# A list scheduler's task priorities: a table of ranks in place of positions from formulas, in an attention and softplus MLP kernel

## The chip, the cores and the metric

The kernel runs on one core of a Trainium2 chip, as one program. The metric is the device time of one execution in microseconds (us), the median of a few runs. The profile is one execution taken by the hardware profiler; it lists every instruction of the engines PE (TensorE matmuls), PEld (its weight loads), DVE (VectorE), ACT (ScalarE), POOL (GpSimd) and SP (the queue that issues nearly all DMAs).

## The reference

Two blocks follow each other. The first is a linear attention with an RMS norm for 8 batches, 8 heads, 576 positions and head size 64; the second is an MLP with softplus over the 4608 tokens that come out.

```python
kv  = einsum('bhsd,bhse->bhde', k, v)
o   = einsum('bhsd,bhde->bhse', q, kv)
a   = o / sqrt(mean(o*o, axis=-1) + 1e-6) * g_norm
x   = a.transpose(0, 2, 1, 3).reshape(4608, 512)
h   = x @ w_in                       # w_in  512 x 2048
g   = max(h, 0) + log1p(exp(-abs(h)))
out = g @ w_out                      # w_out 2048 x 512
```

## The kernel before, in words

**Numbers in three parts.** The MLP's matmuls take operands that are split into three parts (`high`, `low`, `less`), so that three matmuls stand for one. Every operand is split once, by one ACT and two DVE instructions. The weights come in as 64-bit words and are turned into floats first, by six DVE and two ACT instructions for each of 32 pieces (`weight`, lines 409 to 477: `square`, `high1`, `high2`, `mask`, `beyond`, `power`, `rest`, `total`), and are then split (`split_weight`, lines 486 to 538). For the first four of the 16 chunks of the hidden dimension, PE does one step of that split (`less_by_pe`, lines 518 to 521).

**The attention.** `kv_of` (lines 662 to 700) loads k and v of a batch in five pairs and multiplies them on PE (line 691); ACT copies the result (line 699). `rows` (lines 702 to 826) does a tile of 128 tokens: q turned round (on PE at line 771 for batches 0 and 1, on DVE at line 746 for the others), q times kv on PE (`out_rows`, line 715), squares on ACT (line 788), a sum on DVE (`reduce`, line 719), the root on POOL (`root`, lines 722 and 723), and the product on DVE (`norm`, line 727). The first 12 tiles are turned round on PE (`turn_x`, line 733). The first six tiles of x are split at once from PSUM; the others go to DRAM and come back (`x_again`, line 833) before `split` (lines 623 to 649, DVE lines 638 and 641) cuts them.

**The MLP, phase 0.** Tokens go in 12 blocks of 384 (three tiles). A `step` (lines 844 to 892) does one block and one chunk of 128 hidden units: `mm1` (12 matmuls of 384 columns, line 858), softplus and `high` on ACT (lines 880 and 882), `low` and `less` on DVE (lines 869 and 873), and three `mm2` tasks of three matmuls of 512 columns (line 865). Blocks 0 to 3 do chunks 0 to 3, blocks 4 to 11 do chunks 0 to 5: 64 steps.

**The MLP, phases 1 and 2.** The other chunks are done for blocks of 512 tokens in 48 `wide_step`s (lines 1038 to 1161): seven products of six matmuls (line 1060), with copies, additions and softplus on ACT and DVE between them, then eight `mm2` tasks of three matmuls (line 1130). Sums of a phase leave PSUM through ACT (line 925), go to DRAM (`leave`) and come back (`enter`). `leave` of the very last tile of tokens is cut in two halves that ACT (line 915) and DVE (line 918) bring out, with two stores, one issued by SP (line 922) and one by ACT (line 923).

**What sets the order.** Nothing is issued where it stands in the source. Each piece of work is handed to a `Plan` as one of 3795 tasks (`add`, line 79), with its engine, a cost in ns, the tasks that it comes after, the buffers that it takes and gives back, and a position `pos`. `order` (lines 90 to 198) then plays the whole program through: at each turn it takes, for every engine, the tasks that are free to start, keeps those that could start within 0.15 us (`SOON`) of the earliest, and of these chooses the one with the smallest `pos`. The engine whose choice can start first gets it. The list of tasks in order of planned start is the program; each engine works through its part in that order. `pos` is a number from formulas with fitted constants: the step, plus offsets for each kind of task (the lists P0 to P7, lines 250 to 258, `x_pos` at line 657, and the offsets in each helper). Three more rules stand beside `pos`: 64-wide matmuls of one kind (`kv` or `rows`) are kept together and a change of kind is charged on PE; a DMA's `behind` names the `mm1` or first product after which it may be issued; and where PE would stand idle before the seventh `mm1`, the plan puts in a filler matmul of the identity (`warm`, line 1224).

Of the kernel before, what the change touches and what calls it, by code (L numbers as in the profile page):

```python
# [21 lines left out]
DOWN = 1.0 - 2.0 ** -13  # L22
DOWN_G = 1.0 - 0.99 * 2.0 ** -13
E = 1.0 / RADIX


def shaped(x, shape, dtype):
# [28 lines left out]
class Plan:  # L56
# [22 lines left out]
    def add(self, engine, ns, run, after=(), pos=0.0, take=(), give=(), size=0, behind=None, follows=None, kind="all"):  # L79
        pos, behind = round(pos, 4), None if behind is None else round(behind, 4)  # L80
        t = Task(engine, ns, run, [a for a in after if a is not None], pos, list(take), list(give), size)
        for s in t.give:
            s.readers += 1
        self.tasks.append(t)
        t.follows = follows
        t.behind = behind
        t.kind = kind
        return t
# [113 lines left out]
def kernel(  # L202
# [120 lines left out]
    plan = Plan(rings, heirs)  # L323
# [162 lines left out]
    def split_weight(w, part_of, n, dst, ready, pos, of_in, by_pe=False):  # L486
# [28 lines left out]
        def third():  # L515
            nc.scalar.activation(dst.tile[:, 2], d.tile, func=AF.Copy, scale=-E / (1.0 + E))

# [5 lines left out]
        def third_of_bank():  # L523
            nc.scalar.activation(dst.tile[:, 2], bank.tile, func=AF.Copy, scale=-E / (1.0 + E))

# [318 lines left out]
    def step(s):  # L844
# [26 lines left out]
        def less():  # L871
# [7 lines left out]
        mm1s.append((s, a))  # L879
        a = add("ACT", 490, lambda: nc.scalar.activation(new(g, [P, NT]), h.tile, func=AF.Softplus, scale=1.0 + E),  # L880
                [a], s, [g], [h])
# [156 lines left out]
    def wide_step(k):  # L1038
# [47 lines left out]
        def softplus(dst, src):  # L1086
            nc.scalar.activation(dst, src, func=AF.Softplus, scale=1.0 + E)  # L1087

# [76 lines left out]
    def whole_scale(pos):  # L1165

        if not wide:
            scale_done.append(add("DVE", 60, lambda: nc.vector.memset(scale, 1.0 + E), (), pos))
            return
# [5 lines left out]
        scale_done.append(add("ACT", 200, lambda: nc.scalar.activation(  # L1175
            scale, total.tile[:, 0, :1], func=AF.Copy, scale=(1.0 + E) * 2.0 ** -30 / (P * 2 * KF * d_model)), [a], pos, [], [total]))

# [47 lines left out]
                         start=True, stop=True)  # L1225

    plan.spare = ("h", warm, 400, mm1s[6][1])
    for t in plan.order():
        t.run()

# [29 lines left out]
```

## Time and profile before, and how to read it

| | before |
|---|---|
| median of 3 runs | 869.63 us (868.54 to 869.97) |
| span of the profiled execution | 867.5 us |
| PE busy | 853.9 us, 98% |
| DVE busy | 704.4 us, 81% |
| ACT busy | 521.3 us, 60% |
| POOL busy | 76.6 us, 9% |
| HBM read and written | 112.98 and 52.95 MB |
| filler matmuls (line 1224) | 52 |

The span runs from the first to the last instruction of the profiled execution; the time of a run is measured from outside and is some 2 us more. A busy time is the union of an engine's instructions. A matmul's end is modelled, so a busy PE may still work below its pace; the distance between the starts of two matmuls tells more than their length. In a timeline, the bracket at the end of a line gives the engine's idle time before that instruction and what ended it.

### The profile page before, as it was taken

The page shows a single profiled execution, that of the slowest core. Times are in us where ns is not written, and L with a number is a line of the kernel's source. Part 1 is how long each engine was busy: PE and PEld are TensorE (multiplying, and loading weights), DVE is VectorE, ACT ScalarE, POOL GpSimd, SP SyncE. Part 2 cuts the span into 40 slices and gives each one's busy share as a digit, 9 for nine tenths or more (in the row PEclk, how much of TensorE's full clock was granted, in tenths as well). Part 3 has the DMA queues.
Part 4 walks back from the last instruction along what each step waited for, and adds up shares of the span by engine and source line. Part 5 has one row for each costly group of instructions (what it writes and reads, how often), then busy time and mean ns, then how long its engine had stood idle before and what let it go on. Part 6 is the DMA issues. An engine that isn't in the chain of part 4 may idle for free.

```text
span 867.5 us, 17041 instructions
## 1 busy us (share of the span) xinstructions
PE 853.9 (98%) x6464; PEld 760.3 (88%) x6464; DVE 704.4 (81%) x995; ACT 521.3 (60%) x980; POOL 76.6 (9%) x79
## 2 busy tenths in 40 slices
PE   7899999999999999999999999999999999999998
PEld 5678888898888999989999999998999899999996
DVE  7888898888788879798887798878788666788873
ACT  6866664445444467766667655654868555566654
POOL 0342223111113200000000000000000000000000
PEclk9999999999999999999999999999999999999999
DMA  9998998779773655436645546545364752777764
GB/s 278 285 242 230 244 262 255 172 224 234 211 188 114 180 175 166 145 108 209 210 156 164 168 151 205 188 144 170 122 201 140 230 165 91 241 236 241 242 190 126
DMA packets 239778, 167.07 MB, mean 193 GB/s; under 512 B 106320, under 2 KB 198736, under 8 KB 239696
## 3 DMA queue, kind: packets, MB, share of 16 engines
q1 hardware_dynamic: 239392, 165.86, 64.5%
q8 instruction: 50, 0.82, 0.4%
q14 instruction: 32, 0.26, 0.1%
q10 hardware_dynamic: 304, 0.13, 0.1%
HBM read 112.98 MB, written 52.95 MB: 191 GB/s over the span
## 4 chain that ended last, share of the span: by engine, by line
PE 94%; DVE 1%; ACT 1%; POOL 0%; issue 0%; ACTq 0%; DVEq 0%
PE banks L1130 31%; PE banks L1060 28%; PE banks L865 16%; PE banks L858 15%; PE banks L715 2%; PE banks L691 2%; PE banks L733 0%; DVE units L638 0%; DVE half L727 0%; PE banks L1224 0%; POOL roots L723 0%; DVE units L641 0%; DVE roots L719 0%; DVE m L459 0%; ACT units L635 0%
## 5 line engine op out<-in xcount | busy, mean ns | idle before, releaser
L1130 PE MATMUL banks<-pieces,gv 128*128 128x512 f32 x768 | 239.9, 394 | 0.0
L1130 PEld LDWEIGHTS banks<-pieces,gv 128*128 128x128 f32 x768 | 133.5, 189 | 18.4
L1130 PE MATMUL banks<-pieces,g_False 128*128 128x512 f32 x384 | 149.4, 389 | 0.0
L858 PE MATMUL banks<-units,pieces 128*128 128x384 f32 x768 | 145.4, 337 | 0.0
L865 PE MATMUL banks<-pieces,gv 128*128 128x512 f32 x576 | 144.9, 396 | 0.0
L858 PEld LDWEIGHTS banks<-units,pieces 128*128 128x128 f32 x768 | 135.5, 188 | 4.8
L865 PEld LDWEIGHTS banks<-pieces,gv 128*128 128x128 f32 x576 | 106.1, 188 | 20.3
L1060 PEld LDWEIGHTS banks<-units,pieces 128*128 128x128 f32 x840 | 112.8, 190 | 6.8 <-ACT banks L1105 0.4
L1060 PE MATMUL banks<-units,pieces 128*128 128x256 f32 x840 | 117.1, 282 | 0.0
L880 ACT ACTIVATE half<-banks 128x384 f32<-128x384 f32 x64 | 31.4, 491 | 98.2 <-PE banks L858 98.0
L1120 DVE TENSOR_TENSOR gv<-g_True,gv 128x1024 fp32r<-128x1024 f32 x47 | 57.5, 1223 | 37.8 <-ACT gv L1117 37.8
L1130 PEld LDWEIGHTS banks<-pieces,g_False 128*128 128x128 f32 x384 | 72.2, 188 | 15.9
L1060 PEld LDWEIGHTS banks<-units,w 128*128 128x128 f32 x504 | 67.8, 190 | 3.9 <-ACT banks L1105 0.2
L1060 PE MATMUL banks<-units,w 128*128 128x256 f32 x504 | 70.7, 282 | 0.0
L723 POOL TENSOR_TENSOR roots<-roots,half 128x8 f32<-128x8 f32 x36 | 62.3, 1731 | 3.0
L1123 DVE SCALAR_TENSOR_TENSOR g_False<-gv 128x1024 fp32r<-128x1024 f32 x47 | 57.6, 1225 | 1.5
L1109 DVE TENSOR_TENSOR g_True<-banks,g_True 128x512 f32<-128x512 f32 x48 | 33.1, 690 | 30.5 <-PE banks L1060 24.5
L1087 ACT ACTIVATE g_True<-banks 128x256 f32<-128x256 f32 x96 | 36.6, 382 | 32.8 <-PE banks L1060 32.2
L1023 DVE TENSOR_TENSOR units<-loads,units 128x1024 fp32r<-128x1024 f32 x42 | 51.2, 1219 | 6.3 <-ACT units L1020 6.3
L925 ACT ACTIVATE m<-banks 128x512 f32<-128x512 f32 x72 | 42.1, 595 | 19.8 <-PE banks L1130 13.8
L1026 DVE SCALAR_TENSOR_TENSOR units<-units 128x1024 fp32r<-128x1024 f32 x42 | 51.4, 1224 | 1.8
L869 DVE TENSOR_TENSOR gv<-half,gv 128x384 fp32r<-128x384 f32 x64 | 35.4, 553 | 20.6 <-ACT gv L882 19.9
(115 smaller groups left out, 1260.5 us busy)
## 6 DMA issues: line engine op xcount, KB each, us to landing
loads<-x SPq DMA_DIRECT2D x180, 128.0 KB, 2.6
part<-m SPq DMA_DIRECT2D x72, 256.0 KB, 2.9
m<-part SPq DMA_DIRECT2D x72, 256.0 KB, 3.2
loads<-form SPq DMA_DIRECT2D x45, 256.0 KB, 3.2
form<-loads SPq DMA_DIRECT2D x36, 256.0 KB, 3.0
raw<-in_moe_w_in_dram SPq DMA_DIRECT2D x16, 512.0 KB, 4.5
loads<-in_k_dram SPq DMA_DIRECT2D x32, 256.0 KB, 4.1
loads<-in_v_dram SPq DMA_DIRECT2D x32, 256.0 KB, 4.4
```

The source lines that it names most:

```text
L723: nc.gpsimd.tensor_tensor(out=r.tile, in0=r.tile, in1=half, op=ALU.pow)
L858: nc.tensor.matmul(hp, lhsT=w_in.tile[:, i, kd * P:(kd + 1) * P], rhs=xv.tile[:, i, kd], start=(m == 0), stop=(m == 3 * KD - 1))
L865: nc.tensor.matmul(mine[i].tile, lhsT=gv.tile[:, m, i * P:(i + 1) * P], rhs=w_out.tile[:, m], start=(c == cs[0] and m == 0), stop=(c == cs ...
L869: nc.vector.tensor_tensor(out=gv.tile[:, 1], in0=g.tile, in1=gv.tile.bitcast(F32)[:, 0], op=ALU.subtract)
L925: a = add("ACT", 690 if ph == LAST else 600, lambda: nc.scalar.activation(new(ot, [P, d_model]), bank.tile, func=AF.Copy, scale=scale if p ...
L1023: nc.vector.tensor_tensor(out=part_of(1, F32R), in0=xl.tile if m > 1 else xl.tile[:, 0], in1=part_of(0), op=ALU.subtract)
L1026: nc.vector.scalar_tensor_tensor(out=part_of(2, F32R), in0=part_of(1), scalar=-RADIX, in1=part_of(0), op0=ALU.mult, op1=ALU.add)
L1060: nc.tensor.matmul(place(q), lhsT=w[:, m, at:at + P], rhs=dst.tile[:, m, v, kd] if u < 6 else dst.tile[:, m, kd], start=(u == 0 and not m ...
L1087: nc.scalar.activation(dst, src, func=AF.Softplus, scale=1.0 + E)
L1120: nc.vector.tensor_tensor(out=gvt(1, F32R), in0=gt(), in1=gvt(0), op=ALU.subtract)
L1123: nc.vector.scalar_tensor_tensor(out=gt(F32R), in0=gvt(1), scalar=-RADIX, in1=gvt(0), op0=ALU.mult, op1=ALU.add)
L1130: nc.tensor.matmul(mine[i].tile, lhsT=(gvt(m, F32R) if m < 2 else gt(F32R))[:, c, i * P:(i + 1) * P], rhs=outs[c].tile[:, m], start=fresh ...
```

## The change

Before the plan is ordered, each task's `pos` is replaced by a number from a table `RANK` of 3795 integers, one for each task in the order in which the source adds them. The integers are the numbers 0 to 3794, each once. Everything else of the plan stays: costs, dependencies, buffers, the rule of `SOON`, `behind`, `follows`, the rule for 64-wide matmuls and the filler's. The same 3795 tasks come out in another order; only the number of fillers, which the ordering itself puts in, can differ.

```diff
+RANK = [
+    0, 7, 6, 8, 10, 16, 13, 15, 18, 22, 26, 31, 38, 42, 1, 19, 20, 23, 29, 34, 32, 37, 40, 44, 48, 53, 58, 60, 17, 47, 43, 45, 50, 56, 54, 57, 63, 65, 78,
...
+    3774, 3704, 3707, 3718, 3751, 3738, 3752, 3746, 3758, 3747, 3750, 3756, 3760, 3759, 3764, 3762, 3766, 3767, 3769, 3773, 3771, 3776, 3783, 3777, 3781,
+    3779, 3782, 3784, 3787, 3792, 3794, 3780, 3786, 3791, 3785, 3788, 3789, 3793, 3790,
+]
...
     plan.spare = ("h", warm, 400, mm1s[6][1])
+    assert len(RANK) == len(plan.tasks)
+    for t, at in zip(plan.tasks, RANK):
+        t.pos = at
     for t in plan.order():
         t.run()
```

## The prediction

> **What bounds the kernel now.** I read the stages first, to see where any engine has time to lose. The columns are PE, PEld, DVE, ACT and POOL busy (instructions), the granted clock, the DMA share and GB/s.
>
> ```profile
> 0.00:44.00 44.00, 35.66 (x463) 25.53 (x464) 36.70 (x66) 31.27 (x60) 10.10 (x17) 1.00 1.00 281
> 44.00:84.00 40.00, 38.52 (x465) 32.26 (x464) 35.05 (x61) 27.25 (x55) 14.05 (x13) 1.00 0.92 225
> 84.00:137.00 53.00, 53.00 (x545) 46.90 (x544) 47.32 (x82) 31.86 (x63) 13.88 (x14) 1.00 0.87 240
> 137.00:357.00 220.00, 220.00 (x1830) 198.00 (x1829) 185.05 (x319) 116.38 (x230) 38.59 (x37) 1.00 0.68 188
> 357.00:863.70 506.70, 506.70 (x3169) 457.59 (x3167) 399.78 (x470) 314.11 (x573) 0.00 (x0) 1.00 0.57 179
> ```
>
> From 84 to 863.7 us PE has no gap. That this is its pace and not only modelled ends, the starts show: from one wide step to the next it is 10.53 us throughout, 42 matmuls of 256 columns at 0.12 us and 24 of 512 at 0.23. No order makes these shorter. So time can be won or lost in three places: before about 84 us, where PE stands still for 9.8 us and spends about 12 us on fillers (52 at the 0.23 us of a filler among others); in PE's detours to 64-wide matmuls; and after the last matmul.
>
> Next, what feeds PE in the early part. A block of phase 0 can start its first `mm1` when DVE has split its last tile. At blocks 2, 3 and 4 that is just in time (line 641 is the end of the split):
>
> ```profile
> 93.29 0.69 DVE L641 SCALAR_TENSOR_TENSOR units<-units 128x512 fp32r<-128x512 f32 x1
> ...
> 94.17 2.27 PE L858 MATMUL banks<-units,pieces 128*128 128x384 f32 x12
> ...
> 115.55 0.69 DVE L641 SCALAR_TENSOR_TENSOR units<-units 128x512 fp32r<-128x512 f32 x1
> ...
> 115.93 1.40 PE L858 MATMUL banks<-units,pieces 128*128 128x384 f32 x7
> ...
> 136.05 0.68 DVE L641 SCALAR_TENSOR_TENSOR units<-units 128x512 fp32r<-128x512 f32 x1
> ...
> 136.87 0.87 PE L858 MATMUL banks<-units,pieces 128*128 128x384 f32 x4
> ```
>
> So the bound up to 137 us is DVE's queue as much as PE: a PE that came earlier would wait there. At the later blocks the split is done 0.9 to 5.5 us ahead. DVE itself loses time by waiting in its order. Its waits from 35 to 137 us, by what ended them (total, times, longest):
>
> ```profile
> DVE roots L719 <- ACT half L788: 3.9, 4, 1.2
> DVE half L727 <- PE banks L715: 1.6, 3, 0.6
> DVE gv L869 <- ACT gv L882: 1.4, 3, 0.6
> DVE half L727 <- POOL roots L723: 1.3, 4, 0.5
> DVE gv L869 <- PE banks L715: 0.6, 1, 0.6
> ```
>
> With one of 0.4 at line 638 that is 9.2 us in which DVE stood before one instruction while later ones lay ready. An order can win these.
>
> **The change, part by part.** I laid the two programs' instruction orders beside each other, engine by engine. Nearly every task moves, mostly by 2 to 7 places.
>
> *DVE's work ahead of each block: nothing won.* The last split instruction of block 0 stands at place 59 (before: 60), of block 2 at 128 (133), of block 3 at 167 (167), of block 4 at 200 (199). With each instruction at its profiled duration that is 0.9 and 2.9 us less, 0.0, and 0.6 us more. PE's work ahead of the same `mm1` tasks, without fillers and with the detours below, is 2.6 us less for block 2, 0.2 more for block 3 and 1.0 more for block 4. Block 4 is where the account is made: what follows no longer waits for DVE. Its split comes 0.6 us later by this, and 1.0 us less work lies behind it.
>
> *DVE's waits: the gain.* For each of those waits I compared how far the waiting instruction moves on DVE with how far the PE task that feeds it moves on PE. The sums before lines 719 (72.22 us, wait 1.21), 719 (42.31, 0.65), 719 (135.45, 1.00), the `norm`s at 47.92, 54.15, 59.19 and 78.13 (0.38, 0.64, 0.49, 0.59), the split at 51.49 (0.44) and the `low`s at 87.36, 91.55 and 111.77 (0.63, 0.57, 0.58) gain 0.6 us of distance or more, so they go: 7.2 us. Against it, other pairs come closer than their slack: the first `low` of phase 0 goes from place 75 to 67 while its `mm1` stays, which eats 5.0 us where 3.0 were spare (wait about 2); five smaller pairs (reduces, one `low`, one weight split) lose 0.2 to 1.3 us each more than they have, some 2 us in all after what moves together. Net 3 us earlier at block 4. The ends: nothing (new waits take all), and 7.2.
>
> *The first 35 us: nothing.* DMA sets the pace there (share 1.00 to 44 us). The order removes waits of 0.70 and 0.72 us on DVE, but the fourth weight piece still has 4608 KB up to and with it in the DMA order, as before, and lands at 18.2 us, where DVE waited already. k and v of batch 0 have 5376 KB up to their last full load instead of 4864: at 281 GB/s 1.8 us later. PE already waits for that load at 19.30 us (1.69). The sum that needs it stands 2.6 us later on DVE, which covers it.
>
> *Fillers.* 50 instead of 52. They stand only in PE's gaps: cost nothing, while what follows them waits for something else.
>
> *Detours on PE.* A stretch of 64-wide matmuls costs more than its matmuls. Over the 15 such stretches between 84 and 290 us, the starts of the tasks around them fit 0.39 us for a stretch, 0.07 for each change between `kv` and `rows` within it, and 0.47 to 0.49 for each task. The new order has 35 stretches for 32, with 8 inner changes for 11: 3 x 0.39 - 3 x 0.07 = 0.95 us. PE has that much more to do in all; with 1.0 more of it ahead of block 4, what lies behind block 4 is the same within 0.1.
>
> *The end.* Before, the halved last tile is the last thing out; PE ends at 863.7:
>
> ```profile
> 863.75 0.47 ACT L915 ACTIVATE m<-banks,scale 128x256 f32<-128x256 f32 x1 [0.67 <-PE banks L1130]
> 864.24 0.33 SPq L922 DMA_DIRECT2D out_dram<-m  x1
> 864.25 0.48 DVE L918 TENSOR_SCALAR m<-banks,scale 128x256 f32<-128x256 f32 x1 [5.82 <-ACT m L915]
> 864.77 0.35 ACTq L923 DMA_DIRECT2D out_dram<-m  x1
> ```
>
> In the new order another tile's `mm2` is PE's last, one task (0.69 us) after it. On ACT, line 923's issue now stands ahead of that tile's line 925, and it waits for DVE. With E the end of PE: halves out E - 0.66 to E + 0.32, issue to E + 0.7, line 925 (0.69) to E + 1.4, then SP issues a whole store of 256 KB. Before, the last issue is at E + 1.05 with 128 KB (1.7 us to landing in the table of DMA issues). Issue 0.4 us later, landing 0 to 1.1 us longer (256 KB out: 2.8 median): +0.4 to +1.5. I take +0.8, nearer the low end because the queue is empty then.
>
> *Where the cover could go: the wide steps.* In phases 1 and 2 a stall of PE would count in full. The smallest distances on PE between a product and the one that needs its ACT copy or DVE sum stay as they are (0.7 and 1.4 us), and the usual ones grow (median after line 1105: 2.1 to 4.9 us). I cost nothing there.
>
> **Sum.** Start of block 4: waits -3.0, DVE's work +0.6. It started 0.14 us after the end of its split (136.73), block 3 0.32 ahead of it, as a `mm1` reads the split's last part last: a PE that presses on takes another 0.4. Behind block 4 nothing, at the end +0.8. -3.0 + 0.6 - 0.4 + 0.8 = -2.0, with the rounding above -2.1 us. The profiled execution has a span of 867.5, the median of the runs is 869.63; the 2.1 us between them stay. Forecast 865.4 span, **867.5 us**.
>
> **The Trainium skill, one place.** The first 13 matmuls of the trace take 5.92 us, later six take 1.67, though the granted clock reads 1.00 throughout. "TensorE: Matmul & The Clock Gate", in its part on the HAM clock gate, says that the array's clock is halved after an idle window of about 3.4 us and restored after as long a busy one; the slow start agrees. The rule speaks against an order with fewer fillers: by it, a gap of that length would add up to 1.7 us (an estimate from the page). The longest gap on PE before is 1.69 us, and by the trace nothing is added. Such a gap could only come with the late loads of batch 0, a rival below.
>
> **The rivals.**
> - *New waits take the place of the old.* DVE's 9.2 us come again in other places: 869.6 + 0.6 - 0.4 + 0.8 = 870.6. For it: DVE is 0.89 busy from 84 to 137 us, so each instruction that it does early makes another late. Against it: the eleven pairs above.
> - *All the waits go and no new one binds.* -7.2 instead of -3.0 at block 4, but then PE waits earlier: the second `mm2` of step 2 needs DVE's instruction at place 94, which ended at 68.0 us; 2.6 us of the waits lie before it. At 65.7 PE has then done 34.6 us of work and lost 31; before, it had lost 35.8 at 84 us. -4.8 + 0.95 + 0.8 = -3.1: 866.5, at best 865.
> - *Slower: batch 0's k and v.* One mechanism: the 512 KB more ahead of the last load. If SP also issues them late, the 1.8 us grow past the 2.6 of cover; then the first tiles are late, block 0 and DVE with them, nothing else can run, and what the order wins later is lost: +1.8 + 0.6 + 0.8 = 872.8. It decides from a first `out_rows` after about 24 us (now 21.44). If PE then also stood still long enough to fall to the pace of the first fillers (0.43 us instead of 0.23), up to 1.5 us more: 874.3, 0.02 of its chance.
> - *Slower: PE waits in the wide steps.* 0.1 us in each of 48 is +4.8: with the gain 872.4. Against it the distances above.
> - *The change does nothing*: the orders differ in most places, so no chance.
>
> **How the numbers follow.** Forecast 0.42 (own range 866 to 869), new waits 0.27, all go 0.12, batch 0 0.12, wide steps 0.07. The bounds of the unknowns (waits 0 to 7.2, end 0.4 to 1.5) and the rivals give 864.8 (all go at its best) to 872.4; late loads lie outside. A measurement of this kernel can tell about 0.2%, 1.74 us, from no change: faster means under 867.9. The forecast lies close to that: 0.30 of its 0.42 and all of "all go" are faster (0.42), the other 0.12 and 0.20 of "new waits" are the same with 0.02 of the rest (0.34), and 0.24 is slower (0.07 of new waits, 0.12 and 0.07 of the two slower ones, less that 0.02).
>
> **What would show it.** Right: `mm1` of block 4 starts 2 to 3 us before 136.87; DVE's waits from 35 to 137 us sum to about 6 us; PE without gaps after 90 us; line 925 after line 923 at the end, 0.4 us or more later than now after PE's end. Wrong: block 4 at 137 or later, `out_rows` first after 24 us, or any PE wait after 357 us.

## The result, and the profile after

The changed kernel takes **871.37 us** (median; 869.78 to 874.03) where the kernel before takes 869.43 us (868.13 to 871.65): a ratio of 1.0023, 95% interval 1.0016 to 1.0030. It is 1.9 us slower; the forecast was 2.1 us faster. The profiled execution has a span of 869.2 us (before: 867.5). All line numbers behind `order` and the table are 149 higher: 641 is now 790, 858 is 1007, 433 is 582, 719 is 868, 925 is 1074.

The stages of the profile after, in the columns of the stages shown of before:

```profile
0.00:44.00 44.00, 33.96 (x394) 24.49 (x394) 35.02 (x64) 28.69 (x55) 10.69 (x15) 0.96 0.98 271
44.00:84.00 40.00, 39.04 (x473) 33.91 (x474) 34.96 (x63) 28.78 (x59) 14.59 (x14) 1.00 0.94 239
84.00:137.00 53.00, 53.00 (x629) 45.85 (x628) 46.90 (x83) 30.88 (x62) 13.59 (x12) 1.00 0.87 237
```

Behind 84 us PE is without gaps, as before. From 44 to 84 us it stands still for half a microsecond less. Up to 44 us both PE and DVE have done 1.7 us less work than before, DMA brought 271 GB/s instead of 281, and the granted clock was below 1.00. The loss is ahead of 44 us.

The timeline at blocks 3 and 4 (line 790 ends a split, line 1007 is `mm1`):

```profile
115.73 0.65 DVE L790 SCALAR_TENSOR_TENSOR units<-units 128x512 fp32r<-128x512 f32 x1
116.36 2.27 PE L1007 MATMUL banks<-units,pieces 128*128 128x384 f32 x12
...
135.39 1.28 DVE L790 SCALAR_TENSOR_TENSOR units<-units 128x512 fp32r<-128x512 f32 x2
138.15 2.09 PE L1007 MATMUL banks<-units,pieces 128*128 128x384 f32 x11
```

Block 4's split ends at 136.67 us, as before (136.73). But its `mm1` starts 1.5 us later than that, where before it followed at once: PE now comes last, and 1.28 us later than before. The forecast's main sign is refuted here. DVE's waits from 35 to 137 us, of which it said that they would fall from 9.2 to some 6 us, sum to 11.9 us:

```profile
DVE roots L868 <- ACT half L937: 5.6, 5, 1.5
DVE gv L1018 <- ACT gv L1031: 1.9, 5, 0.7
DVE half L876 <- POOL roots L872: 1.7, 3, 0.9
DVE half L876 <- issue: 1.0, 1, 1.0
```

The end of the timeline is as forecast. Line 1074 stands behind line 1072's issue on ACT and waits 1.00 us for it, and from PE's end (864.56) to the end of the span are 4.6 us instead of 3.8:

```profile
863.92 0.47 ACT L1064 ACTIVATE m<-banks,scale 128x256 f32<-128x256 f32 x1 [1.35 <-DMA out_dram<-m]
864.94 0.35 ACTq L1072 DMA_DIRECT2D out_dram<-m  x1
865.40 0.69 ACT L1074 ACTIVATE m<-banks,scale 128x512 f32<-128x512 f32 x1 [1.00 <-DVE m L1067]
866.11 0.33 SPq L1089 DMA_DIRECT2D out_dram<-m  x1
```

So the span's +1.7 us is made of +1.43 at the first `mm1` (45.87 us, before 44.44), -0.15 from there to block 4, -0.43 from block 4 to PE's end, and +0.82 behind PE's end.

### The profile page after: what moved, and what is told of

It is laid out like the page before. It is cut to its first block, busy times and chain, and to the rows that moved or that the text cites. A ratio compares the mean times of both kernels' runs of the same rounds, so it can differ in the third digit from the quotient of the medians.

```text
span 869.2 us, 17010 instructions
## 1 busy us (share of the span) xinstructions
PE 853.6 (98%) x6462; PEld 760.1 (87%) x6462; DVE 695.6 (80%) x995; ACT 515.7 (59%) x980; POOL 79.6 (9%) x79
## 4 chain that ended last, share of the span: by engine, by line
PE 94%; DMA 2%; DVE 1%; ACT 1%; POOL 1%; issue 0%; SPq 0%; ACTq 0%; DVEq 0%
PE banks L1279 30%; PE banks L1209 28%; PE banks L1007 16%; PE banks L1014 16%; PE banks L864 2%; PE banks L840 2%; DMA loads<-in_k_dram 1%; PE banks L882 0%; POOL roots L872 0%; DMA raw<-in_moe_w_in_dram 0%; DMA loads<-in_v_dram 0%; DVE half L876 0%; ACT w L946 0%; PE banks L920 0%; DMA out_dram<-m 0%
## 5 line engine op out<-in xcount | busy, mean ns | idle before, releaser
L1279 PE MATMUL banks<-pieces,gv 128*128 128x512 f32 x624 | 195.0, 394 | 0.0
L1014 PE MATMUL banks<-pieces,gv 128*128 128x512 f32 x576 | 147.9, 397 | 0.0
L1209 PEld LDWEIGHTS banks<-units,pieces 128*128 128x128 f32 x1020 | 134.6, 191 | 6.9 <-ACT g_True L1236 0.2
L1007 PEld LDWEIGHTS banks<-units,pieces 128*128 128x128 f32 x768 | 135.4, 188 | 5.0
L1209 PE MATMUL banks<-units,pieces 128*128 128x256 f32 x1020 | 139.6, 283 | 0.0
L1014 PEld LDWEIGHTS banks<-pieces,gv 128*128 128x128 f32 x576 | 105.4, 188 | 19.3 <-DVE gv L1022 0.3
L1279 PE MATMUL banks<-pieces,g_False 128*128 128x512 f32 x312 | 121.5, 389 | 0.0
L1279 PEld LDWEIGHTS banks<-pieces,gv 128*128 128x128 f32 x624 | 108.4, 189 | 14.6
L1279 PEld LDWEIGHTS banks<-pieces,g_False 128*128 128x128 f32 x312 | 58.7, 188 | 12.9
L1031 ACT ACTIVATE gv<-half 128x384 fp32r<-128x384 f32 x64 | 33.6, 524 | 31.0 <-PE banks L1014 27.7
L1258 DVE TENSOR_TENSOR g_True<-banks,g_True 128x512 f32<-128x512 f32 x48 | 33.0, 688 | 23.4 <-PE banks L1209 11.9
L1074 ACT ACTIVATE m<-banks 128x512 f32<-128x512 f32 x72 | 42.3, 596 | 14.0 <-PE banks L1014 8.8
L1266 ACT ACTIVATE gv<-g_True 128x1024 fp32r<-128x1024 f32 x47 | 49.8, 1060 | 1.3
```

Source lines behind the costliest of these rows:

```text
L1007: nc.tensor.matmul(hp, lhsT=w_in.tile[:, i, kd * P:(kd + 1) * P], rhs=xv.tile[:, i, kd], start=(m == 0), stop=(m == 3 * KD - 1))
L1014: nc.tensor.matmul(mine[i].tile, lhsT=gv.tile[:, m, i * P:(i + 1) * P], rhs=w_out.tile[:, m], start=(c == cs[0] and m == 0), stop=(c == cs ...
L1074: a = add("ACT", 690 if ph == LAST else 600, lambda: nc.scalar.activation(new(ot, [P, d_model]), bank.tile, func=AF.Copy, scale=scale if p ...
L1209: nc.tensor.matmul(place(q), lhsT=w[:, m, at:at + P], rhs=dst.tile[:, m, v, kd] if u < 6 else dst.tile[:, m, kd], start=(u == 0 and not m ...
L1266: nc.scalar.activation(gvt(0, F32R), gt(), func=AF.Copy, scale=DOWN)
L1279: nc.tensor.matmul(mine[i].tile, lhsT=(gvt(m, F32R) if m < 2 else gt(F32R))[:, c, i * P:(i + 1) * P], rhs=outs[c].tile[:, m], start=fresh ...
```

## The experiments

In each of them the table RANK is replaced by a list for each engine, and `order` takes the next task of that list; with the lists of the changed order (e5) the kernel is the changed one, instruction for instruction. A task's number is its place in the source's order, -1 is a filler. So an order can be changed at one place while all others stay. The edits are shown as changes of these lists.

From the timeline of each profile I took four numbers: what DVE waits between its instructions up to 35 us (gaps over 0.06 us), the start of the first `mm1`, and the distances from it to block 4's `mm1` and to PE's end. Ratios are to the kernel before on the same chip; a ratio is estimated from all runs and can differ from the quotient of two medians.

| | ratio (95%) | DVE waits to 35 us | first mm1 | to block 4 | to PE's end |
|---|---|---|---|---|---|
| before | 1 | 4.0 | 44.4 | 92.4 | 819.3 |
| after | 1.0023 (1.0016 to 1.0030) | 5.3 | 45.9 | 92.3 | 818.7 |
| e1 16 fillers first | 1.0010 (1.0001 to 1.0020) | 6.1 | 46.7 | 92.2 | 818.6 |
| e2 end as before | 1.0002 (0.9992 to 1.0012) | 5.2 | 45.8 | 92.2 | 818.7 |
| e3 before, 9 fillers first | 0.9996 (0.9987 to 1.0005) | 5.1 | 45.5 | 92.5 | 819.3 |
| e4 before, changed end | 1.0003 (0.9991 to 1.0014) | 5.2 | 45.9 | 92.4 | 819.3 |
| e5 after again | 1.0021 (1.0011 to 1.0031) | 8.5 | 49.0 | 92.2 | 818.6 |
| e6 early part of before | 0.9997 (0.9987 to 1.0008) | 3.0 | 43.0 | 92.6 | 819.1 |
| e7 early part of after | 1.0091 (1.0076 to 1.0105) | 5.7 | 46.2 | 99.7 | 826.5 |
| e8 k, v first | 1.0058 (1.0046 to 1.0070) | 9.1 | 49.4 | 92.3 | 818.7 |
| e9 two q loads back | 1.0070 (1.0050 to 1.0089) | 8.9 | 50.5 | 92.2 | 818.6 |
| e10 e6, loads moved | 1.0031 (1.0018 to 1.0044) | 8.3 | 49.4 | 92.6 | 819.1 |
| e11 less PE | profile only | 4.3 | 44.5 | 90.0 | 816.9 |
| e12 less DVE | profile only | 5.0 | 45.5 | 92.4 | 819.2 |
| e13 cut at 22 us | 1.0047 (1.0033 to 1.0061) | 7.7 | 48.4 | 92.2 | 818.7 |
| e14 two DVE moves undone | 1.0023 (1.0012 to 1.0034) | 4.7 | 45.3 | 92.2 | 818.6 |
| e15 e6 again | 0.9993 (0.9984 to 1.0002) | 6.1 | 46.7 | 92.7 | 819.1 |
| e16 e6, first mm1 pulled | 1.0026 (1.0015 to 1.0036) | 3.8 | 42.3 | 96.6 | 823.5 |
| e17 before, 512 KB early | 1.0021 (1.0010 to 1.0032) | 5.6 | 45.9 | 92.4 | 819.2 |
| e18 before, 512 KB late | 0.9999 (0.9989 to 1.0009) | 3.4 | 43.7 | 92.4 | 819.2 |

Two things can be read off the columns. The first `mm1` stands at 40.0 to 40.7 us plus DVE's waits in all profiles but e9 and e10 (41.7, 41.1) and e16 (38.6, where it was pulled). And where the first `mm1` moves, block 4 and PE's end move with it, to 0.1 us, in one order. The same early order puts the first `mm1` up to 3.7 us apart from one execution to the next (e6 43.0, e15 46.7), so a single profile does not compare two early parts; many runs do. As the distance to PE's end and the stretch behind it are the same, to 0.1 us, in all profiles of an order, the span of each run tells its own first `mm1`. By this estimate it stands at 46.4 us as the mean of 57 runs with the changed early order (after, e1, e2, e5), and at 44.9 in 127 runs of the kernel before: the changed early part costs 1.5 us, give or take 0.3.

**The clock: e1 and e3.** The first theory was about the granted clock. In the profile after, one filler fewer stands ahead of the first `kv`, PE has nothing from 6.34 to 8.26 us, and the clock falls to half:

```profile
8.00:9.00 1.00, 0.74 (x17) 0.65 (x17) 0.97 (x3) 0.67 (x1) 0.00 (x0) 0.86 1.27 296
...
11.00:12.00 1.00, 1.00 (x6) 0.50 (x4) 0.93 (x3) 1.00 (x3) 0.00 (x0) 0.50 0.82 206
```

```diff
 PE, after (e1)
-    -1 x 12, 372, -1, 387,
+    -1 x 16, 372, -1, 387,
 PE, before (e3)
-    -1 x 13, 372, -1, -1, 375,
+    -1 x 9, 372, -1, -1, 375,
```

> The changed order with 16 fillers instead of 12 ahead of PE's first kv task, nothing else moved. Theory (clock): in the changed order PE has nothing from 6.3 to 8.3 us, and the granted clock reads 0.50 from about 8.7 to 12.1 us; over its 22 runs the mean clock goes from 0.995 to 1.000 and the time with it, 873 to 869.8 us. Four more fillers of 0.43 us close the gap: clock 1.00, some 1.4 us won, 869.8 to 870.3 us. Rival (loads): the first tiles are late because k and v of batch 0 land later in the new DMA order, which the fillers do not touch: time as the changed kernel's, 871.4 us within 0.4.

> The order of before with 9 fillers instead of 13 ahead of the first kv task, so that PE has a gap of about 2.6 us there; nothing else is moved, and batch 0's loads keep their places. Theory (clock): the granted clock falls to 0.50 for some 3.4 us in most runs (mean 0.998 or less) and the time rises by 1 to 2 us to 870.5 to 871.5. Rival (loads): nothing in front of the first kv task matters, 869.4 us within 0.4.

Measured: e1 870.81 us, 0.6 under the changed kernel's first median, with intervals that overlap: it lies between its two expectations and meets neither. e3 870.01 us against 869.99 of before, though its mean clock lay at 0.998 (0.9987 in the runs of before beside it). A lower clock in the first 20 us did not cost e3 anything, and the profile of e2, with a clock of 1.00 throughout, has the first `mm1` where the profile after has it (45.82, 45.87). As the main cause the theory falls: a lower clock goes along with a late start. A share of some tenths in the 1.9 us stays possible, for by the spans of its runs e1's first `mm1` stands at 45.9 us, 0.6 ahead of the other runs with the changed early order.

**The end: e2 and e4.**

```diff
 PE, after (e2)
-    3778, 3790, 3784
+    3778, 3784, 3790
 ACT, after (e2)
-    3788, 3791, 3794, 3785
+    3788, 3785, 3791, 3794
 SP, after (e2)
-    3789, 3793, 3786
+    3789, 3786, 3793
```

e4 is the reverse on the order of before.

> The changed order with its end as before: the halved tile's mm2 is PE's last task again, and line 925's (now 1074) whole store stands ahead of the two halves on ACT and SP. Theory (end): the stretch from PE's end to the end of the span goes from 4.64 back to about 3.8 us, and the time falls by 0.85 us to 870.5 us. Rival (the end is hidden or given back in the last store): within 0.3 us of the changed kernel, 871.1 to 871.6.

> The order of before with the end of the changed one: the halved tile's mm2 one task ahead of the last, line 925 behind line 923 on ACT, the whole store last on SP. Theory (end): +0.85 us, 870.3 us. Rival (hidden): 869.4 us within 0.3. Its early part is that of before, so its list of clocks also tells how often the order of before falls below 1.000: by the theory of the clock hardly ever, by the rival as often as the changed one (21 of 22 runs).

Measured: e2 870.25 us, e4 870.10 us. By the traces the stretch behind PE's end is 3.8 us in before and e2 and 4.6 in after and e4: the end is worth 0.8 us, near the 0.85 expected. The medians agree in sign (e2 1.1 us under the changed kernel's first median, e4 0.1 over that of before), but with intervals of 0.1% on each side neither would show it alone. Of e4's 12 runs 7 had a clock below 1.000, of the changed kernel's 22 runs 21: neither "hardly ever" nor as often.

**Which part is slow: e5, e6, e7, e15.** The orders are cut at the first `mm1` (task 1024).

```diff
 every engine (e6, e15; the end as in e2)
+    the tasks that stand ahead of 1024 in the order of before, as there
+    what is left, as in the changed order
```

> The changed order, instruction for instruction, once more, so that the runs of this set stand beside it on the same chip. Both theories: 1.9 us above the kernel before, as in its first runs (ratio 1.0023); first mm1 at 45.9 us, block 4's at 138.1, PE's end at 864.5, or all of them later by one and the same shift where the first loads come later.

> All engines and SP in the order of before up to the first mm1 (44 us), then what is left in the changed order; the end with the halved tile last, as before. Theory (early part): what the changed order lost, it lost ahead of the first mm1, and a shift there goes through to the end one to one, as the run with 9 fillers showed (1.06 us later at the first mm1, 1.08 at block 4, 1.10 at PE's end). So: first mm1 at 44.4, block 4's at 136.7, PE's end 863.0, span 866.8: 2.2 us under the changed kernel and 0.5 under the one before. Rival (new waits of DVE from 45 to 137 us hold block 4 whenever PE comes): block 4 at 137.7 or later, PE's end 864.2, and only the 0.85 us of the end won.

> The reverse: the changed order up to the first mm1, then what is left in the order of before, with its end. Theory (early part): first mm1 at 45.9, block 4 at 138.3, PE's end at 865.1, time 1.4 us over the kernel before. Rival (new waits of DVE from 45 to 137 us, which this order does not have): the lateness is taken up by block 4, 137.0 there, time within 0.4 us of the kernel before.

> The run with the early part and the end of before and the changed order between, once more, to narrow its interval: first mm1 at 43 to 46 us as DMA has it, from there 92.63 us to block 4 and 819.05 us to PE's end, against 92.43 and 819.27 in the order of before. By that 0.2 us under the kernel before; by the first measurement 0.6 under it; within 0.2% in either case.

Measured: e5 871.32, e6 869.22, e15 869.25, e7 877.37 us. With the early part of before the loss is gone: 2.1 us under the changed kernel, of which the end is 0.8. By the ratios alone, e6 and e15 (0.9997 and 0.9993) do not stand apart from e2 (1.0002), which has only the end of before; the estimate from the spans of the runs above does tell the two early parts apart. In e6's profile the first `mm1` is at 43.0 instead of the 44.4 expected, and block 4 at 135.6; the distance is 92.6, near the theory's 92.3. e7 was a miss for both theories: behind its seam 11.2 us pass between the first two `mm1` (before: 5.2), and DVE waits 12.8 us from 35 to 84 us (before: 5.5). The changed order had done five weight steps more ahead of the seam, but not the sums and splits that the order of before has done by then. It tells nothing of the early part's price.

**What sets the pace from the first `mm1` on: e11 and e12.** These decide the forecast's main step. On the order of before, e11 leaves out PE work, e12 DVE work:

```diff
+    for at in (1085, 1115, 1123, 1153):        # e11: four mm2
+        plan.tasks[at].run = lambda: None
+    for at in (102, 116, 131, 145, 160):       # e12: five mask steps
+        plan.tasks[at].run = lambda: None
```

> The order of before with four mm2 tasks of blocks 1 to 3 left out (three matmuls each, 0.69 us: 2.77 us of PE between 91 and 130 us; the sums miss their share). The distance from the first mm1 to block 4's is 92.43 us in all profiles of that order. Theory (PE's pace sets it: PE waits only 1.3 us there after the first mm1): the distance falls by 2 us or more, to 89.7 to 90.4. Rival (as the prediction had it, DVE's queue bounds as much, and a PE that comes earlier waits at the splits): it falls by 0.5 us at most, with new waits of PE.

> The order of before with one of the six DVE steps (mask, 0.69 us) of five weight pieces left out between 65 and 123 us, 3.4 us of DVE; the weights lose the clearing of their smallest values. Theory (PE's pace): block 4's split is done up to 3 us earlier, and its mm1 comes at most 0.6 us earlier: the distance from the first mm1 stays at 91.8 to 92.4. Rival (prediction: what DVE saves ahead of block 4, block 4 gains): the distance falls to 89.5 to 90.

First e11, then e12, first `mm1` and block 4's:

```profile
44.51 2.27 PE L1007 MATMUL banks<-units,pieces 128*128 128x384 f32 x12
...
134.54 4.36 PE L1007 MATMUL banks<-units,pieces 128*128 128x384 f32 x24
```

```profile
45.51 2.27 PE L1007 MATMUL banks<-units,pieces 128*128 128x384 f32 x12
...
137.13 0.68 DVE L790 SCALAR_TENSOR_TENSOR units<-units 128x512 fp32r<-128x512 f32 x1
137.95 4.36 PE L1007 MATMUL banks<-units,pieces 128*128 128x384 f32 x24
```

Take 2.77 us from PE, and block 4 comes 2.40 us earlier. Take 3.4 us from DVE, and it comes at the same time; DVE waits 7.4 us from 84 to 137 us instead of 5.2. Even the split does not end earlier, expected had been up to 3 us: it ends 0.14 us ahead of its `mm1`, as in before. That "just in time" is no sign of a DVE that is late. DVE's sums wait for ACT's squares of PE's products (5.6 us of waits from 35 to 137 us in the profile after), so the split is itself fed at PE's pace.

**Which part of the first 44 us: e8, e9, e14, e13.** Waits of DVE up to 35 us, first before, then after (the two lines on the weights' loads):

```profile
DVE m L433 <- DMA raw<-in_moe_w_in_dram: 1.3, 1, 1.3
DVE m L433 <- DMA g<-in_moe_w_out_dram: 0.5, 1, 0.5
```

```profile
DVE m L582 <- DMA raw<-in_moe_w_in_dram: 2.9, 2, 1.6
DVE m L582 <- DMA g<-in_moe_w_out_dram: 0.9, 1, 0.9
```

DVE waits 3.8 us for weights instead of 1.8. Up to 20 us DMA brings 256 GB/s instead of 283: 0.54 MB less, some 1.9 us. In the other profiles with the early order of before it is 262 to 289 (e17, which adds a transfer, left out), in those with the changed one 247 to 261. The last full load of k of batch 0 is issued later, first before, then after:

```profile
12.21 0.42 SPq L680 DMA_DIRECT2D loads<-in_k_dram  x1
```

```profile
17.64 0.47 SPq L829 DMA_DIRECT2D loads<-in_k_dram  x1
```

By the traces it lands at 22.45 us instead of 19.17, and the fourth weight piece at 19.16 instead of 18.22. I tried to find the moves that do it.

```diff
 SP, after (e8; kv tasks, copy and out_rows moved up on PE and ACT)
-    382, 383, 414, 42, 400, 377, 379, 56
+    382, 383, 377, 379, 414, 42, 400, 56
 SP, after (e9; their turns and copies moved back on PE and ACT)
-    386, 458, 380, 376, 461, 28, ... 377, 379, 56
+    386, 380, 376, 28, ... 377, 379, 458, 461, 56
 DVE, after (e14)
-    30, 31, 24, ... 46, 48, 49, 38
+    24, 30, 31, ... 38, 46, 48, 49
 every engine (e13): as e6, but cut behind the first two out_rows (22 us)
```

> The changed order with the last pair of full k and v loads of batch 0 one place behind the tails, ahead of two q loads and a weight piece (4352 KB up to it instead of 5376), and on PE and ACT the kv tasks, the copy and the first out_rows moved up accordingly; DVE's order untouched. Theory (late loads of batch 0 make the first mm1 late): out_rows first at about 22 us instead of 25.4, first mm1 at 44.5 to 45, time 1 us or more under the changed kernel. Rival (DVE's own order: its first reduce stands at place 33, behind weight work that ends at 27 us, so earlier rows wait for DVE): out_rows early, first mm1 at 45.5 or later, time within 0.4 us of the changed kernel.

> The changed order with two small q loads (tile 4's first parts, four DMAs of 64 KB) taken back on SP from places 6 and 9 to behind the last full k and v load, and their turns on PE and copies on ACT behind them; DVE's order untouched. In the profiles so far the first mm1 stands at 40.5 us plus the time that DVE waits in the first 35 us (4.0 to 5.2 us in the order of before, 5.2 to 8.5 in the changed one), and DMA brings 262 to 289 GB/s up to 20 us against 247 to 261. Theory (small loads in front keep SP's first weights and k and v back): GB/s up to 20 us at 265 or more, DVE's waits up to 35 us under 5, first mm1 by 45.3, time 1 us or more under the changed kernel (870.3 or less). Rival (DVE's early order makes the waits: it wants the third and fourth weight piece ahead of other work): GB/s as it may be, DVE's waits stay at 5.2 or more, time within 0.5 us of the changed kernel.

> The changed order with two moves on DVE undone: the last split steps of the first and third weight piece stand again ahead of the next piece's first steps, as before. Nothing moves on any other engine or on SP. Theory (loads): DVE's waits for weights up to 35 us get shorter by what is put ahead of them, but the wait for ACT (0.7 to 2.6 us in the profiles of the order of before) comes in their place: first mm1 within 0.7 us of 46.3, time within 0.7 us of 871.4. Rival (these two moves are the cause of the lateness): first mm1 by 45, time 870 or less.

> All engines and SP in the order of before only up to the first two out_rows (22 us) instead of up to the first mm1 (44 us), then what is left in the changed order; the end as before. What the two orders differ in ahead of the first mm1 is thereby cut in two. Theory (the first 22 us: the order of the first twenty loads): DVE waits 4 to 5 us up to 35 us, first mm1 at 44 to 45.5, time 869.2 to 869.8. Rival (22 to 44 us: in the changed order DVE puts the fifth weight piece ahead of the first reduces): first mm1 at 46 or later, time 870.3 or more, as the changed order with its end put back.

Measured: e8 874.91, e9 875.81, e14 871.35, e13 873.07 us. e14 is clear: the two moves on DVE are not the cause. In e8 and e9 the time missed both expectations; e13 is on its rival's side (870.3 or more), but far beyond. All three lost more than they could show. In e8 the first `out_rows` came at 22.9 us as expected, but SP stood still for buffers of k and v, the next weight piece came late and DVE waited 5.1 us for it. In e9 the rate rose to 266 GB/s, yet the rows came at 28.8 us and DVE waited 4.6 us for them. In e13 the rate was 284, and DVE waited 3.2 us for an ACT task behind the seam. In these runs, rows early or loads dense alone did not bring the first `mm1` forward, and a move on two queues left a third waiting.

**A delay alone: e17 and e18.** So nothing is moved, only a transfer added to the order of before:

```diff
+    more = dram.tile([P, 2 * d_model], F32, name="more")
+
+    def with_more(run=plan.tasks[28].run):       # e18: 112
+        nc.sync.dma_start(out=more, in_=q[7].rearrange("h s d -> (h s d)")[:2 * P * d_model].rearrange("(p f) -> p f", p=P))
+        run()
+
+    plan.tasks[28].run = with_more               # e18: 112
```

> The order of before with one more transfer of 512 KB (from q into a DRAM buffer that nobody reads), issued by SP ahead of the third weight piece at about 9.6 us: the 512 KB that the changed order has more ahead of batch 0's last full load, without any move. Theory (what DVE waits in the first 35 us goes through to the end): 512 KB at 281 GB/s are 1.87 us; DVE's waits up to 35 us grow by 1.5 to 2.5, the first mm1 comes at 46 to 47.5 us, and the time is 871.2 to 872. Rival (the prediction's step: later k and v are covered by what stands in front of the first reduces on DVE): first mm1 within 0.5 us of what that order has otherwise (43 to 46), time within 0.5 us of before.

> The same 512 KB, issued behind the first mm1 (ahead of the eighth weight piece, at 47 us) in the order of before. Both theories: nothing, 869.8 us within 0.6, as the loads there land long before they are wanted; it is the control that the transfer by itself, its write included, is not what costs. Were the time up by 1 us or more here too, the early run would tell nothing of the first 35 us.

DVE's waits up to 35 us, e17 and then e18:

```profile
DVE m L582 <- DMA raw<-in_moe_w_in_dram: 3.6, 2, 2.1
```

```profile
DVE m L582 <- DMA raw<-in_moe_w_in_dram: 1.3, 1, 1.3
```

Measured: e17 872.18 us, e18 869.28, both against 869.28 of before. e17's ratio is 1.0021, some 1.8 us with an interval of 0.9 to 2.8 (2.9 by the medians, above the 871.2 to 872 expected); e18's is 0.9999. In e18's trace the added transfer is issued at 60.9 us, ahead of the ninth weight piece, and not at the 47 us that was expected; it is behind the first `mm1` all the same. So 512 KB more ahead of the third weight piece cost about what they take on the queue and reach the end, and the same transfer behind the first `mm1` costs nothing that shows. e17's own first `mm1`, 45.9 us, is just below the 46 to 47.5 expected and within what that order shows elsewhere; its time and the 3.6 us of waits for weights carry the verdict. It prices late weights above all: against the profile of before the third weight piece lands 2.5 us later, the last full load of k of batch 0 only 0.9. Whether late k and v alone are covered, as the forecast held, no run tells.

**Mixed orders that might beat both: e10 and e16.** Both start from e6.

```diff
 SP (e10; DVE: 30, 31 ahead of 24)
-    0, 370, 382, 14, 371, 374, 373, 386, 383, 428, 28
+    0, 370, 14, 371, 374, 373, 386, 28, 382, 383, 428
 PE (e16)
-    512, 464, 422, 478, -1 x 6, 1024, 1032, 82, 469, 501, 1040, 96
+    422, 512, 464, -1, 1024, 478, 1032, 82, 501, 1040, 469, 96
 ACT (e16)
-    513, 465, 423, 479, 426, 79, 89, 81
+    423, 79, 513, 465, 426, 479, 81, 89
 DVE (e16)
-    438, 439, 78, 86, 466, 424, 480, 425, 80, 87, 88
+    78, 438, 424, 425, 439, 466, 86, 80, 87, 88, 480
```

> The early part and end of before with the changed order between (as in the run that did this), and two more moves: on SP the tail loads of batch 0 and the q load of tile 3 go behind the third weight piece, on DVE the first weight's last split goes behind the two first steps of the third piece, as in the changed order. Theory (loads): the third weight piece lands 1 to 2 us earlier, DVE's wait for ACT at its place 14 goes, DVE waits 0.5 to 1 us less up to 35 us than in the run without these moves, and the time is 868.5 us, 1.2 under the kernel before. Rival (PE and ACT then wait for what went back): no gain or a loss against the 869.2 us of that run.

> The same, with the first mm1 pulled forward: on PE the third tile's turn_x ahead of the next q turn and the first mm1 right behind the first out_rows of the next block, without fillers; on ACT and DVE that tile's three split steps ahead of weight work and of reduces that nothing waits for. In the run without this, PE stands 1.4 us and fills ahead of the first mm1, and the split stands behind 1.6 us of such DVE work. Theory (PE's pace decides from the first mm1 on): the first mm1 comes 1.5 to 2.5 us earlier, PE then waits some of it away at the next sums; at block 4 0.5 to 1.5 us stay, time 868.0 to 869.0. Rival (DVE, which has no gap from 27 to 53 us in that run, sets block 1): everything is back at the old time by block 1, 869.3 us.

Measured: e10 872.72, e16 871.37 us, both slower than e6. e10 fell like e8: SP stood 3.4 us for buffers of k and v, and DVE waited for weights (4.2 us) and for ACT. In e16 the first `mm1` did come 2 us earlier against DVE's waits, but the third came 7.8 us behind it instead of 5.9, and by block 4 the distance had grown by 4 us. This points to DVE's queue as the pace between 27 and 53 us, where DVE in e6 has no gap over 0.3 us: work put ahead there makes other work late. The pace of PE is shown only for the stretch behind it (e11 leaves out work from 91 us on). e6 with e15 is the best order found, 0.3 to 0.7 per mille under the kernel before, but both intervals hold 1: no gain is shown.

## Why the prediction was wrong

1. *What bounds the kernel.* "The bound up to 137 us is DVE's queue as much as PE" is the step that failed first. It was read from splits that end where `mm1` starts; e12 shows that they end there because PE feeds them. Of the 2.8 us that were to be won up to block 4, 0.15 came behind the first `mm1`. The trace of before had the counter-evidence. These are all of PE's waits that it names between 44 and 137 us, 1.3 us together, so shorter waits could not win 3 us there:

```profile
PE banks L733 <- DVE half L727: 0.5, 1, 0.5
PE banks L715 <- ACT w L797: 0.4, 1, 0.4
PE banks L771 <- DVE half L727: 0.2, 1, 0.2
PE banks L691 <- DVE units L638: 0.2, 1, 0.2
```

2. *DVE's waits, -3.0.* Of the 7.2 us in eleven named waits 4.8 went. But at ten other places the waits grew by 7.4 us together, where about 4 had been allowed for; the sum went up from 9.2 to 11.9. By e12 neither counts at block 4.
3. *DVE's work, +0.6.* The instructions ahead of block 4's split take 0.3 us more, near the forecast. Not foreseen: without its waits, DVE gets through them in 3.1 us less (last section). That kept the split in time in spite of the longer waits.
4. *PE presses on, -0.4.* PE came 1.5 us after the split; void.
5. *The first 35 us: nothing.* This term, put at nothing, made most of the loss: without it, the other parts of the span add up to +0.2. It measured +1.43 at the first `mm1` in the two profiles, +1.8 as a mean of profiles (44.9 us in eight with the early order of before, 46.7 in five with the changed one), and +1.5 by the spans of the runs. The forecast counted bytes alone. It had 1.8 us for the later k and v and wrote them off against a later reduce; the load landed 3.3 us later, as SP also issued it 5.4 us later, and that is more than the 2.6 us of cover. It took the fourth weight piece to land as before; it landed 0.9 us later, and DVE waited 3.8 us for weights instead of 1.8. "DVE waited already" was no reason for it to wait no longer. How much of the 1.5 us is k and v and how much the weights stays open.
6. *Fillers and the clock.* 50 for 52 cost nothing that e1 and e3 could establish. (All 52 together are nearer 15 than 12 us, as the first 13 alone take 5.92.) But a gap longer than the 1.69 us of before did come (1.92 us at 6.34), and half clock with it for 3.4 us (8.7 to 12.1). "TensorE: Matmul & The Clock Gate" of the Trainium skill, in its part on the HAM clock gate, gives about 3.4 us for its window, and the length agrees. By that part of the Trainium skill the clock halves after an idle window of that length; here shorter gaps were enough. Of the ten profiles whose first gap at this place had 1.83 to 3.5 us, seven fell to half clock right behind it (e7 with 1.83 us, after with 1.92) and three did not (e11 with 1.91, e16 with 2.14, e10 with 2.87); of the ten with 1.75 us or less none did. So the length alone does not decide, and what else does, no run settles.
7. *Detours and what lies behind block 4: nothing.* Measured -0.43, where it was to be "the same within 0.1"; with the work ahead of it -0.58 from the first `mm1` to PE's end. No run shows where the 0.4 comes from.
8. *The end, +0.8.* Right: +0.82, by the mechanism named.
9. *The wide steps: nothing.* Right: PE has no gap behind 84 us.

The rival "batch 0's k and v" named its decision point, a first `out_rows` after 24 us. It came at 25.42, and the rival's +1.8 is near the 1.5 that the start cost; it got a chance of 0.12. Its mechanism, that SP issues these loads late as well, is seen in the trace, but e8, which brought them forward, did not win the time back. The rival's 872.8 missed the 0.6 us that the order does win behind the first `mm1`: 1.5 - 0.6 + 0.8 gives +1.7, against +1.94 measured. What stays open is which of the early moves makes the loads less dense: small q loads in front (e9 raised the rate by 10 GB/s by taking two of them back), the 1.4 us that SP waits at 3.8 us for an earlier transfer to land, or its waits for buffers of k and v. No run separated them.

## What to carry to other kernels

An instruction that ends just ahead of its consumer may be fed by that consumer's engine: before an order is credited with a shorter wait on one engine, add up what the bounding engine itself waits in that stretch, because shorter waits can win no more. In a start-up phase in which transfers are the pace, bytes put ahead of a needed load can reach the end in full (here 512 KB cost 0.9 to 2.8 us), so compare two orders by the bytes ahead of each early load and by when it is issued, for every engine that waits for one. And the queues of an order hang together: of three ways to join parts of the two orders, two (e7, e13) were slower than both and one (e6) was as fast as before; moving a few loads or tasks on some of the queues (e8, e9, e10, e16) was slower each time.

## What the hardware showed that was not expected

DVE starts an instruction earlier when it does not need the result of the one in front. In the timeline of before:

```profile
28.76 0.69 DVE L638 TENSOR_TENSOR units<-banks,units 128x512 fp32r<-128x512 f32 x1
29.49 0.69 DVE L641 SCALAR_TENSOR_TENSOR units<-units 128x512 fp32r<-128x512 f32 x1
30.10 0.68 DVE L727 TENSOR_TENSOR half<-banks,roots 128x512 f32<-128x512 f32 x1
```

Line 641 needs line 638's result and starts 0.04 us after its end; line 727 needs neither and starts 0.08 us before the end of line 641. Over all such pairs without another wait the medians are +0.035 and -0.082 us, in both kernels. So a dependent neighbour costs 0.117 us. Before, 65 of the pairs ahead of block 4's split are dependent, after, 30: 35 x 0.117 = 4.1 us. What is seen is 3.1 us: without its waits over 0.06 us, DVE is 122.1 us on the way to the end of that split before, and 118.9 after. In the whole kernel the dependent pairs fall from 311 to 205. "Perfetto Trace Analysis" of the Trainium skill, in its part on optimizing Scalar and DVE operations, says that the half of an instruction's latency in which the write is acknowledged overlaps the next instruction; the -0.082 us agrees, while the dependent neighbours here, at +0.035 us, show no overlap. In this kernel the gain is idle behind 84 us, where PE has no gap; whether it pays where DVE bounds, no run here shows.
